# A fused attention, rotation and expert kernel on one core: the order of its first batch's theta, token-mixing and attention work changed, with weights staged by halves and some softmax sums kept in PSUM

## Chip, cores and metric

One core of one Trainium2 chip runs the whole program. The metric is device time in microseconds (us), the median of several executions. TensorE, VectorE, ScalarE, GpSimd and SyncE are called PE, DVE, ACT, POOL and SP in the rows.

## The reference

Three stages follow each other, for 4 batches of 576 tokens: a sparse attention of 8 heads (4 local, 4 strided), a rotation and mixing block, and four experts with causal attention. The change touches only the first two, and their order.

```python
scores = scale * np.matmul(q, k.transpose(0, 1, 3, 2))
scores = np.where(masks, scores, -1000000000.0)
attn = np.exp(scores - np.max(scores, axis=-1, keepdims=True))
attn = attn / (np.sum(attn, axis=-1, keepdims=True) + 1e-09)
x = np.matmul(attn, v)
...
theta = x @ w_theta
zr, zi = x * np.cos(theta), x * np.sin(theta)
y = np.einsum('ts,bsd->btd', w_tok_r, zr) + np.einsum('ts,bsd->btd', w_tok_i, zi)
u = x + y
x = u + np.maximum(u @ w_ch, 0.0)
```

The weights of the mixing block arrive as 64-bit floats.

## The kernel before

Every large product is done as three matmuls on a high and a low part of both factors (`mm3`, lines 252 to 255), so each weight is first split. `load64` (line 116) does it for `wth` (theta), `wtk` (token mixing) and `wch` (channel mixing): a chunk of 128 rows comes by DMA into a free part of the activation buffer X[3], ACT takes its magnitude (line 130), DVE builds the 32-bit pattern in three steps (lines 131 to 133) in X[2], ACT writes the high part (line 98) and DVE or POOL the low part (lines 100, 102). `wtk` has nine chunks and is loaded in two column halves.

Attention goes by pairs of heads, four per batch, each in three groups (`attn_pair`, line 161): scores on PE into a PSUM tile `s`, softmax on DVE and ACT (with ACT summing as it takes exponentials in the groups that `per_tile` names; DVE adds 1e-9 at line 203 and takes the reciprocal at 204), the division on POOL (205), a transposition `tp`, its copy `pt`, and the product with v into `av`, which is copied into X.

Then, per batch and column half h: `theta` (line 263) makes five tiles `th`, of twelve matmuls each, with two PSUM buffers; DVE takes a tile out into `cs` (lines 276, 277), ACT the absolute value (278) and, after the last tile, the cosines and sines (283, 284), for which it loads another table than for exponentials. `rotate` (286) multiplies with the transposed x and splits into `zhi` (ACT in the first batch) and `zlo` (POOL, 314). `tokens` (318) makes four tiles `y` of 27 matmuls per half. `channels` follows in the next batch.

The attention of batch b+1 is spread between these steps of batch b (`next_pair`, line 376; the main loop is lines 382 to 417). Within an engine a scheduler orders the instructions by readiness in a timeline of its own, starting from program order; each engine then works its list strictly in that order. `tc.issue_after(i)` puts the block's instructions behind instruction i on i's own engine only. All loads go through SP's one list.

In the first batch the order before is: attention of batch 0, with `wth` loaded after its first two pairs; theta half 0; rotation half 0; first half of `wtk`; theta half 1; rotation half 1; second half of `wtk`; pairs 0 and 1 of batch 1; `y` of half 0; `wch` and pair 2; pair 3; `y` of half 1.

Of the kernel before, what the change touches and what calls it, by code (L numbers as in the profile page):

```python
# [12 lines left out]
F32 = mybir.dt.float32  # L13
# [28 lines left out]
def fused_kernel(ctx: ExitStack, tc: tile.TileContext, ql, kl, vl, qs, ks, vs, wth, wtk, wch, wqk, wvg, wo, out):  # L42
# [73 lines left out]
    def load64(dst, src, kt, n0, n1, scale=1.0):  # L116
# [6 lines left out]
        slots = S // n  # L123
        for c in range(kt):
            raw = X[3].bitcast(U32).rearrange("p (a c) s -> p a (c s)", a=2)[:, c // slots % 2, :]
            raw = raw.rearrange("p (a s) -> p a s", a=slots)[:, c % slots, :2 * n].rearrange("p (n t) -> p n t", t=2)
# [6 lines left out]
            nc.vector.scalar_tensor_tensor(w, up, 0x80000000, w, op0=ALU.bitwise_and, op1=ALU.bitwise_or)  # L133
            split_w(hi[:, c, n0:n1], lo[:, c, n0:n1], st, scale, nc.vector if c % 3 == 1 else nc.gpsimd)

# [25 lines left out]
    def attn_pair(b, pair, ps1, apl, deep):  # L161
# [6 lines left out]
        for g, (j0, j1) in enumerate(groups):  # L168
# [13 lines left out]
            sm = apl.tile([128, 4], F32, tag="sm", name=f"sm_{b}_{pair}_{g}")  # L182
            p = apl.tile([128, 3 * LK], F32, tag="p", name=f"p_{b}_{pair}_{g}")
# [7 lines left out]
            if per_tile(b, pair, g):  # L191
                nc.vector.tensor_reduce(mx[:rm, :n], tiles(s), axis=AX.X, op=ALU.max, negate=True)
                nc.scalar.activation(mx[:rm, :n], mx[:rm, :n], AF.Copy, scale=SCALE)
                for i in range(n):
                    nc.scalar.activation(p[:rm, i * kw:(i + 1) * kw], s[:rm, i * kw:(i + 1) * kw], AF.Exp,
                                         bias=mx[:rm, i:i + 1], scale=SCALE, accum_out=sm[:rm, i:i + 1])
# [6 lines left out]
            nc.vector.tensor_scalar_add(sm[:rm, :n], sm[:rm, :n], 1e-9)  # L203
# [59 lines left out]
    def theta(b, h):  # L263
# [4 lines left out]
        for t in range(NT):  # L268
# [5 lines left out]
            cs = rp.tile([128, 2, 256], F32, tag="cs", name=f"cs_{b}_{h}_{t}")  # L274
# [85 lines left out]
    with tc.tile_pool(name="ps0", bufs=2, space=PSUM) as ps0, tc.tile_pool(name="ain0", bufs=9) as ain0, \  # L360
            tc.tile_pool(name="apl0", bufs=5) as apl0:
        for pair in range(4):
            load_pair(0, pair, ain0, 4, 4)
        attn_pair(0, 0, ps0, apl0, 2)
        attn_pair(0, 1, ps0, apl0, 2)
        load64(wth_s, wth, 4, 0, DM, INV2PI)
        for pair in range(2, 4):
            attn_pair(0, pair, ps0, apl0, 2)
    zu = ph1.enter_context(tc.tile_pool(name="zu", bufs=4))
# [12 lines left out]
    for b in range(B):  # L382
# [4 lines left out]
        rotate(b, 0)  # L387
        if b > 0:
            next_pair(b, 1)
        else:  # L390
            load64(wtk_s, wtk, 9, 0, HALF)
            load_pair(1, 0, ain, 2, 2)
        theta(b, 1)
        if b > 0:
            next_pair(b, 2)
        rotate(b, 1)
        if b == 0:
            load64(wtk_s, wtk, 9, HALF, S)
# [9 lines left out]
        if b == 0:  # L408
            next_pair(b, 0)
            next_pair(b, 1)  # L410
        tokens(b, 0)
        if b == 0:
            with tc.issue_after(sins[0, 1]):
                load64(wch_s, wch, 4, 0, DM)
# [312 lines left out]
```

## Time and profile before

| | us |
|---|---|
| median of 3 runs | 582.23 |
| lowest, highest | 581.08, 583.97 |
| the profiled execution | 579.94 |
| its span | 578.2 |
| PE busy in the span | 542.3 (94%) |
| DVE busy | 412.3 (71%) |
| ACT busy | 316.2 (55%) |
| POOL busy | 234.3 (41%) |
| mean granted clock of PE | 0.968 |

A row of a timeline gives an instruction's start, its length, its tile and, in brackets, how long the engine stood idle before it and what ended that. The clock column of a window is the granted clock of PE as a share of 2.4 GHz; 0.50 is the lower level, 1.2 GHz. A busy share over the whole span hides that the first fifth of it is worked differently from the rest.

### The profile page before, as it was taken

What the parts mean: (1) busy time and instruction counts of PE and PEld (TensorE: products, weight loads), DVE (VectorE), ACT (ScalarE), POOL (GpSimd) and SP (SyncE); (2) the same over time, 40 slices, a digit from 0 to 9 for tenths busy, and PEclk for the clock granted to TensorE, in tenths of its full rate; (3) what the DMA queues carried; (4) which work ended last, traced back from release to release, by engine and by line L of the source; (5) the groups of instructions that cost most, each with busy time, mean ns of one, the idle gap of its engine ahead of it and who ended that gap; (6) DMA issues with size and microseconds to landing.
All of it is one profiled execution on the core that took longest, in us unless ns stands there. A gap on an engine that the chain in (4) does not pass through costs nothing.

```text
span 578.2 us, 12507 instructions
## 1 busy us (share of the span) xinstructions
PE 542.3 (94%) x4560; PEld 508.1 (88%) x4560; DVE 412.3 (71%) x1205; ACT 316.2 (55%) x882; POOL 234.3 (41%) x314
## 2 busy tenths in 40 slices
PE   6787689899999999999999999899999999999996
PEld 6677579799999999999999999898989899899985
DVE  4896897995687456776255553488987888879882
ACT  5754966533536217254142550287678667866873
POOL 3532383650145211445104460365364534534452
PEclk9957969899999999999999999999999999999999
DMA  9557634221322013110100010100001001100012
GB/s 306 191 166 226 224 123 133 95 69 64 95 86 85 2 32 126 37 38 2 56 1 1 1 57 0 37 2 2 1 12 43 31 1 43 34 9 12 32 42 82
DMA packets 18660, 37.53 MB, mean 65 GB/s; under 512 B 2200, under 2 KB 9544, under 8 KB 18600
## 3 DMA queue, kind: packets, MB, share of 16 engines
q1 hardware_dynamic: 18600, 36.74, 19.6%
q8 instruction: 36, 0.59, 0.4%
q14 instruction: 24, 0.20, 0.1%
HBM read 32.01 MB, written 4.72 MB: 64 GB/s over the span
## 4 chain that ended last, share of the span: by engine, by line
PE 67%; DVE 14%; ACT 9%; DMA 5%; issue 2%; POOL 2%; SPq 0%; ACTq 0%; POOLq 0%; DVEq 0%
PE y L253 6%; PE y L254 6%; PE y L255 6%; PE tp L559 3%; PE th L253 3%; PE th L255 3%; PE th L254 3%; PE g L253 2%; PE g L254 2%; PE s L180 2%; PE g L255 2%; PE pq L253 2%; PE o L583 2%; PE s L533 2%; PE av L231 2%
## 5 line engine op out<-in xcount | busy, mean ns | idle before, releaser
L253 PE MATMUL y<-wtk_hi,zhi 128*128 128x288 f32 x288 | 86.9, 303 | 1.6 <-DVE cs L277 0.6
L254 PE MATMUL y<-wtk_lo,zhi 128*128 128x288 f32 x288 | 85.6, 298 | 1.0 <-POOL wtk_lo L100 1.0
L255 PE MATMUL y<-wtk_hi,zlo 128*128 128x288 f32 x288 | 84.5, 296 | 0.0
L314 POOL TENSOR_TENSOR zlo<-cs,zhi 128x512 fp32r<-128x512 f32 (+1 forms) x40 | 49.5, 1249 | 66.0 <-DVE zhi L311 42.1
L556 POOL TENSOR_SCALAR p<-p,sm,gt 128x256 f32<-128x256 f32 (+1 forms) x64 | 45.2, 709 | 57.2 <-DVE sm L554 38.9
L205 POOL TENSOR_TENSOR p<-p,sm 128x288 f32<-128x288 f32 (+2 forms) x48 | 32.3, 682 | 81.0 <-DVE sm L204 60.1
L549 ACT ACTIVATE p<-s,nm 128x128 f32<-128x128 f32 (+2 forms) x96 | 49.5, 517 | 14.8 <-DVE nm L538 10.0
L253 PEld LDWEIGHTS y<-wtk_hi,zhi 128*128 128x128 f32 x288 | 54.2, 188 | 3.0 <-DVE X L329 1.1
L249 POOL TENSOR_TENSOR x_lo<-X,x_hi 128x576 fp32r<-128x576 f32 x24 | 37.0, 1546 | 45.9 <-DVE x_hi L247 35.9
L254 PEld LDWEIGHTS y<-wtk_lo,zhi 128*128 128x128 f32 x288 | 54.2, 188 | 1.3 <-POOL wtk_lo L100 1.1
L255 PEld LDWEIGHTS y<-wtk_hi,zlo 128*128 128x128 f32 x288 | 53.9, 188 | 0.0
L253 PE MATMUL th<-wth_hi,x_hi 128*128 128x256 f32 (+1 forms) x160 | 50.2, 314 | 2.4 <-DVE cs L277 1.5
L538 DVE TENSOR_REDUCE nm<-s 128x1 f32<-128x128 f32 (+2 forms) x96 | 44.4, 469 | 5.2 <-PE s L536 3.9
L254 PE MATMUL th<-wth_lo,x_hi 128*128 128x256 f32 (+1 forms) x160 | 47.5, 297 | 0.0
L255 PE MATMUL th<-wth_hi,x_lo 128*128 128x256 f32 (+1 forms) x160 | 47.4, 297 | 0.0
L180 PEld LDWEIGHTS s<-k,q 128*108 128x108 f32 (+1 forms) x320 | 41.6, 201 | 6.0 <-issue 4.5
L180 PE MATMUL s<-k,q 128*108 128x54 f32 (+2 forms) x320 | 43.4, 279 | 3.4 <-DMA k<-in_kl 3.3
L253 PE MATMUL pq<-x_hi,wqk_hi 128*128 128x288 f32 x128 | 39.9, 312 | 0.7 <-DVE q L505 0.7
L212 ACT COPY pt<-tp 96x384 f32<-96x384 f32 (+2 forms) x44 | 20.8, 473 | 35.4 <-PE tp L208 35.2
L568 DVE TENSOR_TENSOR ptlo<-tp,pthi 128x128 fp32r<-128x128 f32 (+4 forms) x80 | 38.0, 478 | 2.5 <-ACT pthi L567 1.9
L253 PE MATMUL g<-u_hi,wch_hi 128*128 128x288 f32 x128 | 39.4, 308 | 0.2 <-DVE X L351 0.2
L254 PE MATMUL pq<-x_lo,wqk_hi 128*128 128x288 f32 x128 | 37.9, 296 | 0.0
(156 smaller groups left out, 1732.7 us busy)
## 6 DMA issues: line engine op xcount, KB each, us to landing
X<-in_wtk SPq DMA_DIRECT2D x18, 288.0 KB
q<-in_qs SPq DMA_DIRECT2D x8, 594.0 KB
q<-in_ql SPq DMA_DIRECT2D x8, 576.0 KB
out_t<-X SPq DMA_DIRECT2D x32, 144.0 KB
v<-in_vl SPq DMA_DIRECT2D x24, 144.0 KB
k<-in_kl SPq DMA_DIRECT2D x8, 304.0 KB
k<-in_ks SPq DMA_DIRECT2D x8, 288.0 KB
X<-in_wth SPq DMA_DIRECT2D x4, 512.0 KB
```

The costliest lines, as they stand in the source:

```text
L180: nc.tensor.matmul(s[:rm, i * kw:i * kw + w], qt[:, j0 + i, :], kt[:, k0:k0 + w], start=False, stop=i == n - 1)
L205: nc.gpsimd.tensor_tensor(tiles(p), tiles(p), each(sm), op=ALU.mult)
L212: copy(pt[:kw, :n * rm], tp[:kw, :n * rm])
L249: eng.tensor_tensor(lo, x, f(hi), op=ALU.subtract)
L253: nc.tensor.matmul(ps, ahi, bhi, start=first, stop=False)
L254: nc.tensor.matmul(ps, ahi, blo, start=False, stop=False)
L255: nc.tensor.matmul(ps, alo, bhi, start=False, stop=last)
L314: nc.gpsimd.tensor_tensor(lo, zf, f(hi), op=ALU.subtract)
L538: nc.vector.tensor_reduce(nm[:w, t + ci:t + ci + 1], s[:w, :c1 - c0], axis=AX.X, op=ALU.max, negate=True)
L549: nc.scalar.activation(p[:w, c0:c1], scs[ci][:w, :c1 - c0], AF.Exp, bias=nm[:w, t:t + 1], scale=1.0, accum_out=acc)
L556: eng.tensor_scalar(p[:w, :kn], p[:w, :kn], sm[:w, t:t + 1], gt[:w, t, e:e + 1], op0=ALU.mult, op1=ALU.mult)
L568: nc.vector.tensor_tensor(dst(ptlo), src, f(dst(pthi)), op=ALU.subtract)
```

## The change

Theta's weights come in two halves of 256 columns: the first is loaded after pair 1 of batch 0 and ahead of the loads of pairs 2 and 3, the second after those pairs. They are staged in X[1], so that `wtk` in X[3] no longer waits for them; every chunk now has one of four slots of its own. `wch` is loaded by halves too. Theta half 1 directly follows theta half 0; for four of its five tiles `cs` lies in X[1]. `load64` returns the last DVE step, and the first pair of batch 1 is put behind it on DVE and behind the last `zhi` of half 0 on ACT. In the 13 groups of batches 0 and 1 in which ACT sums, the sums go into four spare columns of the PSUM tile `s` (nine groups of batch 0, four of batch 1); DVE reads them there.

```diff
-    def load64(dst, src, kt, n0, n1, scale=1.0):
+    def load64(dst, src, kt, n0, n1, place, scale=1.0):
...
-            raw = X[3].bitcast(U32).rearrange("p (a c) s -> p a (c s)", a=2)[:, c // slots % 2, :]
-            raw = raw.rearrange("p (a s) -> p a s", a=slots)[:, c % slots, :2 * n].rearrange("p (n t) -> p n t", t=2)
+            raw = X[place].bitcast(U32)[:, c % 4, :2 * n].rearrange("p (n t) -> p n t", t=2)
...
-            nc.vector.scalar_tensor_tensor(w, up, 0x80000000, w, op0=ALU.bitwise_and, op1=ALU.bitwise_or)
+            got = nc.vector.scalar_tensor_tensor(w, up, 0x80000000, w, op0=ALU.bitwise_and, op1=ALU.bitwise_or)
...
+        return got.ins
...
+            ss = s[:, 384:388] if per_tile(b, pair, g) else sm
...
-                                         bias=mx[:rm, i:i + 1], scale=SCALE, accum_out=sm[:rm, i:i + 1])
+                                         bias=mx[:rm, i:i + 1], scale=SCALE, accum_out=ss[:rm, i:i + 1])
...
-            nc.vector.tensor_scalar_add(sm[:rm, :n], sm[:rm, :n], 1e-9)
+            nc.vector.tensor_scalar_add(sm[:rm, :n], ss[:rm, :n], 1e-9)
...
-            cs = rp.tile([128, 2, 256], F32, tag="cs", name=f"cs_{b}_{h}_{t}")
+            if (b, h) == (0, 1) and t < 4:
+                cs = X[1][:, t, :512].rearrange("p (a c) -> p a c", a=2)
+            else:
+                cs = rp.tile([128, 2, 256], F32, tag="cs", name=f"cs_{b}_{h}_{t}")
...
-        for pair in range(4):
+        for pair in range(2):
             load_pair(0, pair, ain0, 4, 4)
         attn_pair(0, 0, ps0, apl0, 2)
         attn_pair(0, 1, ps0, apl0, 2)
-        load64(wth_s, wth, 4, 0, DM, INV2PI)
+        load64(wth_s, wth, 4, 0, 256, 1, INV2PI)
+        for pair in range(2, 4):
+            load_pair(0, pair, ain0, 4, 4)
         for pair in range(2, 4):
             attn_pair(0, pair, ps0, apl0, 2)
+        load64(wth_s, wth, 4, 256, DM, 1, INV2PI)
...
-        rotate(b, 0)
-        if b > 0:
+            rotate(b, 0)
             next_pair(b, 1)
+            theta(b, 1)
+            next_pair(b, 2)
         else:
-            load64(wtk_s, wtk, 9, 0, HALF)
+            theta(b, 1)
+            rotate(b, 0)
+            ready = load64(wtk_s, wtk, 9, 0, HALF, 3)
             load_pair(1, 0, ain, 2, 2)
-        theta(b, 1)
-        if b > 0:
-            next_pair(b, 2)
         rotate(b, 1)
         if b == 0:
-            load64(wtk_s, wtk, 9, HALF, S)
+            load64(wtk_s, wtk, 9, HALF, S, 3)
...
         if b == 0:
-            next_pair(b, 0)
+
+            with tc.issue_after(ready), tc.issue_after(turns[0, 0]):
+                next_pair(b, 0)
             next_pair(b, 1)
         tokens(b, 0)
         if b == 0:
             with tc.issue_after(sins[0, 1]):
-                load64(wch_s, wch, 4, 0, DM)
+                for n0 in range(0, DM, 256):
+                    load64(wch_s, wch, 4, n0, n0 + 256, 3)
```

Names in the orders below carry batch, pair or half, and group or tile: `q_0_2` is q of batch 0, pair 2; `X1`, `X2` and `X3` are the buffers of batches 1 to 3, used for staging. SP's list from the loads of pair 2 of batch 0 on, before:

```order
L152 DMA q_0_2_146<-in_qs 128x1188
L153 DMA k_0_2_147<-in_ks 128x576
L157 DMA v_0_2_0_150<-in_vs 54x512
L157 DMA v_0_2_1_152<-in_vs 54x512
L157 DMA v_0_2_2_154<-in_vs 54x384
L152 DMA q_0_3_156<-in_qs 128x1188
L153 DMA k_0_3_157<-in_ks 128x576
L128 DMA X3_101<-in_wth 128x1024 x2
L157 DMA v_0_3_0_160<-in_vs 54x512
L157 DMA v_0_3_1_162<-in_vs 54x512
L157 DMA v_0_3_2_164<-in_vs 54x384
L128 DMA X3_101<-in_wth 128x1024 x2
```

and of the change:

```order
L126 DMA X1_99<-in_wth 128x512 x4
L151 DMA q_0_2_354<-in_qs 128x1188
L152 DMA k_0_2_355<-in_ks 128x576
L156 DMA v_0_2_0_358<-in_vs 54x512
L156 DMA v_0_2_1_360<-in_vs 54x512
L156 DMA v_0_2_2_362<-in_vs 54x384
L151 DMA q_0_3_364<-in_qs 128x1188
L152 DMA k_0_3_365<-in_ks 128x576
L126 DMA X3_101<-in_wtk 128x576 x4
L126 DMA X1_99<-in_wth 128x512
L156 DMA v_0_3_0_368<-in_vs 54x512
L126 DMA X1_99<-in_wth 128x512
```

A half of `wth` moved ahead of pair 2, four chunks of `wtk` ahead of everything that waits for `wth`, and the second half of `wth` behind them. DVE's list where theta's first tile is taken out (`cs_0_0_0`), before:

```order
L131 TENSOR_SCALAR X2_100<-X2_100 128x288
L132 SCALAR_TENSOR_TENSOR X2_100<-X3_101,X2_100 128x288
L133 SCALAR_TENSOR_TENSOR X2_100<-X3_101,X2_100 128x288
L276 TENSOR_SCALAR cs_0_0_0_619<-th_0_0_0_606 128x256
L276 TENSOR_SCALAR cs_0_0_1_636<-th_0_0_1_623 128x256
L131 TENSOR_SCALAR X2_100<-X2_100 128x288
L277 SCALAR_TENSOR_TENSOR cs_0_0_0_619<-cs_0_0_0_619,th_0_0_0_606 128x256
L100 TENSOR_TENSOR wtk_lo_114<-X2_100,wtk_hi_113 128x288
L192 TENSOR_REDUCE mx_1_0_0_1019<-s_1_0_0_1014 128x3
L277 SCALAR_TENSOR_TENSOR cs_0_0_1_636<-cs_0_0_1_636,th_0_0_1_623 128x256
```

and of the change:

```order
L130 SCALAR_TENSOR_TENSOR X2_100<-X3_101,X2_100 128x288
L131 SCALAR_TENSOR_TENSOR X2_100<-X3_101,X2_100 128x288
L129 TENSOR_SCALAR X2_100<-X2_100 128x288
L280 TENSOR_SCALAR cs_0_0_0_647<-th_0_0_0_634 128x256
L100 TENSOR_TENSOR wtk_lo_114<-X2_100,wtk_hi_113 128x288
L130 SCALAR_TENSOR_TENSOR X2_100<-X3_101,X2_100 128x288
L280 TENSOR_SCALAR cs_0_0_1_664<-th_0_0_1_651 128x256
L281 SCALAR_TENSOR_TENSOR cs_0_0_0_647<-cs_0_0_0_647,th_0_0_0_634 128x256
L131 SCALAR_TENSOR_TENSOR X2_100<-X3_101,X2_100 128x288
L193 TENSOR_REDUCE mx_1_0_0_1043<-s_1_0_0_1038 128x3
L199 TENSOR_REDUCE mx_1_0_1_1065<-s_1_0_1_1060 128x3
```

Five chunks of `wtk` (steps into X2) stood ahead of `cs_0_0_0` before; now eight do and the ninth has begun, and the maxima `mx_1_0_0` and `mx_1_0_1` of batch 1 stand behind the last step of the ninth. ACT's list behind the sines of theta half 0, before:

```order
L201 ACTIVATE p_1_1_1_1139<-p_1_1_1_1139 128x288
L130 ACTIVATE X2_100<-X3_101 128x288
L313 CAST zhi_0_0_0_704<-cs_0_0_0_619 128x512
L193 ACTIVATE mx_1_2_0_1368<-mx_1_2_0_1368 108x4
L98 ACTIVATE wtk_hi_113<-X2_100 128x288
L212 COPY pt_1_0_2_1076<-tp_1_0_2_1072 96x384
L130 ACTIVATE X2_100<-X3_101 128x288
L313 CAST zhi_0_0_1_712<-cs_0_0_1_636 128x512
L201 ACTIVATE p_1_1_2_1160<-p_1_1_2_1160 128x288
L130 ACTIVATE X2_100<-X3_101 128x288
L313 CAST zhi_0_0_2_720<-cs_0_0_2_653 128x512
L212 COPY pt_1_1_0_1130<-tp_1_1_0_1126 96x384
```

and of the change:

```order
L128 ACTIVATE X2_100<-X3_101 128x288
L98 ACTIVATE wtk_hi_113<-X2_100 128x288 x2
L282 ACTIVATE X1_99<-X1_99 128x256
L317 CAST zhi_0_0_0_823<-cs_0_0_0_647 128x512
L98 ACTIVATE wtk_hi_113<-X2_100 128x288
L282 ACTIVATE X1_99<-X1_99 128x256
L317 CAST zhi_0_0_1_831<-cs_0_0_1_664 128x512
L128 ACTIVATE X2_100<-X3_101 128x288
L282 ACTIVATE X1_99<-X1_99 128x256
L317 CAST zhi_0_0_2_839<-cs_0_0_2_681 128x512
L98 ACTIVATE wtk_hi_113<-X2_100 128x288
```

The exponentials (`p`), copies (`pt`) and maxima of batch 1 that stood between the `zhi` of half 0 have moved behind the sines of half 1, which follow without a table load between; ACT loads two tables fewer in all. On PE the first two score tiles of batch 1 (`s_1_0_0`, `s_1_0_1`) stand between the second and the third tile of theta half 0 before and after; from there to the last tile of theta half 1 no other work of batch 1 is left on PE, where before much of three pairs stood; the other ten groups' scores now stand among the matmuls of `y`. The number of instructions is the same on PE; DVE has 29 more, ACT 14, POOL 3 and SP 8.

## Rows read from the trace of the kernel before

**Rows 1.** Windows of the four stages: busy us (x instructions) by engine, clock, DMA.

```profile
0.00:38.00 38.00, 28.09 (x293) 23.74 (x294) 26.62 (x78) 25.36 (x102) 16.38 (x31) 0.85 0.62 212
38.00:88.50 50.50, 40.00 (x311) 36.76 (x312) 42.94 (x116) 32.69 (x101) 24.08 (x25) 0.77 0.64 199
88.50:131.50 43.00, 39.56 (x348) 37.39 (x348) 36.79 (x75) 21.83 (x48) 23.40 (x19) 0.96 0.29 94
131.50:578.20 446.70, 434.68 (x3614) 410.20 (x3612) 305.94 (x938) 236.32 (x634) 170.40 (x240) 1.00 0.11 34
```

**Rows 2.** Windows inside them: the same columns.

```profile
0.00:20.00 20.00, 15.64 (x149) 14.14 (x149) 10.68 (x41) 11.94 (x54) 7.11 (x22) 1.00 0.88 305
28.00:37.70 9.70, 7.96 (x88) 5.95 (x86) 8.77 (x19) 7.29 (x17) 3.41 (x4) 0.50 0.30 96
37.70:54.00 16.30, 12.98 (x61) 12.38 (x62) 11.75 (x28) 7.04 (x22) 5.17 (x5) 0.60 0.91 277
63.60:71.90 8.30, 4.12 (x50) 3.23 (x48) 6.03 (x16) 8.26 (x21) 2.82 (x4) 0.96 0.72 233
71.90:81.40 9.50, 7.06 (x41) 6.43 (x42) 9.46 (x24) 7.05 (x23) 8.96 (x9) 0.50 0.32 83
```

**Rows 3.** TensorE timeline: start, us, instruction [idle before <- what ended it].

```profile
37.72 0.58 PE L253 MATMUL th<-wth_hi,x_hi 128*128 128x256 f32 x1 [0.84 <-ACT X L238]
...
46.52 2.15 PE L180 MATMUL s<-k,q 128*128 128x96 f32 x12 [2.46 <-DMA k<-in_kl]
...
49.51 0.58 PE L253 MATMUL th<-wth_hi,x_hi 128*128 128x256 f32 x1 [0.84 <-DVE cs L277]
...
54.63 0.80 PE L180 MATMUL s<-k,q 128*128 128x96 f32 x6
...
71.94 0.91 PE L231 MATMUL av<-pt,v 96*64 96x64 f32 x12 [2.97 <-ACT pt L212]
...
88.50 0.38 PE L253 MATMUL y<-wtk_hi,zhi 128*128 128x288 f32 x1
...
94.40 0.29 PE L253 MATMUL y<-wtk_hi,zhi 128*128 128x288 f32 x1
...
94.53 0.30 PE L254 MATMUL y<-wtk_lo,zhi 128*128 128x288 f32 x1
```

**Rows 4.** ScalarE timeline: a table load, sines of theta half 1, what follows.

```profile
62.88 1.28 ACT L283 ACT_TABLE_LOAD   x1
...
95.60 0.51 ACT L283 ACTIVATE cs<-cs,halfpi 128x256 f32<-128x256 f32 x1
...
99.16 0.64 ACT L130 ACTIVATE X<-X 128x512 f32<-128x512 f32 x1
```

**Rows 5.** SyncE timeline: transfers issued.

```profile
32.32 4.52 SPq L128 DMA_DIRECT2D X<-in_wtk  x4
...
37.87 0.43 SPq L153 DMA_DIRECT2D k<-in_kl  x1
```

**Rows 6.** VectorE groups by form, 0 to 130 us: xcount | busy us, mean ns.

```profile
L132 DVE SCALAR_TENSOR_TENSOR X<-X,X 128x288 uint32<-128x288 uint32 x18 | 8.8, 490 | 0.1
...
L203 DVE TENSOR_SCALAR sm<-sm 108x4 f32<-108x4 f32 x8 | 6.2, 781 | 0.0
...
L132 DVE SCALAR_TENSOR_TENSOR X<-X,X 128x512 uint32<-128x512 uint32 x8 | 6.0, 755 | 0.0
...
L203 DVE TENSOR_SCALAR sm<-sm 108x3 f32<-108x3 f32 x4 | 3.8, 950 | 0.0
...
L203 DVE TENSOR_SCALAR sm<-sm 128x3 f32<-128x3 f32 x14 | 3.1, 226 | 1.8 <-ACT p L195 1.6
```

**Rows 7.** Lines 203 and 276: duration ns min/median/max, first and last start us.

```profile
L203 DVE TENSOR_SCALAR sm<-sm x48: 129/162/1737, 8.8 to 264.8; 128x3 f32<-128x3 f32 x24, 108x4 f32<-108x4 f32 x16, 108x3 f32<-108x3 f32 x8
...
L276 DVE TENSOR_SCALAR cs<-th x40: 382/423/426, 47.4 to 318.9; 128x256 f32<-128x256 f32 x32, 64x256 f32<-64x256 f32 x8
```

**Rows 8.** Tile cs, line 314: the low part of z on GpSimd, ns min/median/max.

```profile
L314 POOL TENSOR_TENSOR zlo<-cs,zhi x10: 723/1354/1943, 71.2 to 116.8; 128x512 fp32r<-128x512 f32 x8, 128x256 fp32r<-128x256 f32 x2
```

More of the change, by code (lines that the diff above doesn't have):

```diff
@@ L114, in new_split @@
         return tuple(pool.tile([128, kt, n], F32R, name=f"{name}_{part}") for part in ("hi", "lo"))
-    def load64(dst, src, kt, n0, n1, scale=1.0):
+    def load64(dst, src, kt, n0, n1, place, scale=1.0):
         hi, lo = dst
         n = n1 - n0
-        slots = S // n
         for c in range(kt):
-            raw = X[3].bitcast(U32).rearrange("p (a c) s -> p a (c s)", a=2)[:, c // slots % 2, :]
-            raw = raw.rearrange("p (a s) -> p a s", a=slots)[:, c % slots, :2 * n].rearrange("p (n t) -> p n t", t=2)
+            raw = X[place].bitcast(U32)[:, c % 4, :2 * n].rearrange("p (n t) -> p n t", t=2)
             st = X[2][:, c % 4, :n]
```

## Prediction

> **What bounds the kernel now.** I read the span in slices and the granted clock first, then windows by stage, then the timeline of PE at the borders of the stages, and last the groups and timelines of the engines on which PE waits. PE is busy for most of the span, so I count what it loses: its idle time, plus half of its busy time in stretches where the clock is at the lower level (work at 1.2 GHz takes twice as long as at 2.4).
>
> By stage [rows 1, 2]: from 0 to 38 us (attention of batch 0) PE idles 9.9 us and has 7.96 us at clock 0.50, so it loses 9.9 + 4.0 = 13.9. From 38 to 88.5 (theta, three pairs of batch 1, until `y` starts) it idles 10.5 us; 12.98 us (37.7 to 54) and 7.06 us (71.9 to 81.4) lie mostly at the lower level, which costs 10.0: together 20.5. The first window's mean of 0.60 takes in idle time, so I count all of it. From 88.5 to 131.5 (first `y`) it idles 3.4 us and loses 0.04 x 39.6 = 1.6 to the clock: 5.0. Up to 131.5 that is 39.4 us lost and 131.5 - 39.4 = 92.1 us of work at full speed. Behind 131.5 PE idles 12.0 of 446.7 us at clock 1.00, and no line changes there. The change adds nothing to PE, so all that it can bring lies in these 39.4 us, and more than half in the theta stage.
>
> What holds PE there [rows 3, 4]: theta starts at 37.72; its third tile waits for DVE to empty a PSUM buffer (line 277), until 49.51; ahead of it a score tile of batch 1 waits 2.46 us for its `k` (46.52). Then score tiles of batch 1 and theta alternate, behind softmax work on DVE and ACT; the table for theta's sines is loaded at 62.88; `y` begins only at 88.50, with the second half's sines later still, at 95.60.
>
> **The change part by part.** *Stage A, until theta starts.* The first half of `wth` (4 x 256 KB = 1.05 MB) now goes ahead of the loads of pairs 2 and 3; at the 305 GB/s of the first 20 us [rows 2] that delays them by 3.4 us. In exchange half of the conversion of `wth` moves to where DVE was busy for 10.68 of 20 us, and away from 28 to 37.7, where DVE was busy for 8.77 of 9.7. Bounds: 2 us earlier to 3.4 later. I take 0: the end that is nearest to a row is the relief of DVE, which was nearly full just ahead of theta, but pair 3 comes later.
>
> *Third theta tile.* Before, four chunks of `wtk` were issued at 32.32, for 4.52 us, ahead of `k` at 37.87 [rows 5]. Now these four chunks (1.18 MB, 3.9 us at 305 GB/s) leave before the second half of `wth`, and more conversions stand ahead of `cs_0_0_0` on DVE. The last chunk of `wth` should land near 43.5 and take about 3 us to be converted and to let the tile go: 46.5 in place of 49.51. Bounds: 45.6 (little behind the landing) to 49.5 (no change). I take 46.5.
>
> *Theta to its sines.* From 49.51 to the table load at 62.88 were 13.4 us, with softmax of batch 1 on DVE and ACT between. Behind the hold some 3.3 us of it are gone from DVE, and theta tiles follow each other: I take about 10, so the table load comes near 56. A table load and the sines of both halves, 1.28 + 3.56 us for the ten of the second half [rows 4], end near 61. Four `zhi` on ACT, among conversions that wait, take about 5.4 by the spacing of the same work before: 66.6. `zlo` on POOL, 1.35 us each [rows 8], follows them. The first two tiles of `y` are 54 matmuls x 0.13 us (two starts, 94.40 and 94.53, [rows 3]) = 7 us; they should start near 64 and, waiting for `zlo` and for `wtk`, end near 73. That is as if `y` began whole at 66.5. So the stage runs from 38 to 66.5 = 28.5 us. Its work: 120 theta matmuls x 0.117 us (0.13 x 256/288) = 14, and 3 for two score tiles (0.80 each [rows 3]) and some transposes: 17. It loses 11.5, where before it lost 20.5.
>
> *First y stage.* What is left is 92.1 - 24.1 (stage A's 38 - 13.9) - 17 = 51.0 us of work, with more of batch 1's attention in it than before. DVE bounds this: it was busy 26.62 + 42.94 + 36.79 = 106.4 us up to 131.5 [rows 1]. Halves instead of whole rows add about 3: a step of 288 columns takes 490 ns and one of 512 takes 755 [rows 6], so two of 256 (estimated at 0.45 each) cost 0.15 us more, sixteen times, and the shorter operations of 16 chunks the rest. That makes 109, so by 124.5 DVE may idle for 15 us only, if it is to end there; before it idled for 25. I take 7 us lost by PE, against 5.0 before; bounds 3 (DVE out of the way) to 14 (the whole gain used up). The stage ends at 66.5 + 51.0 + 7 = 124.5, which is **7.0 us earlier** than 131.5.
>
> *Sums in PSUM.* Thirteen of line 203's instructions read PSUM instead of SBUF: eight of 128x3, four of 108x4, one of 108x3 [rows 6]. On SBUF their times run from 129 to 1737 ns; the nearest row with a PSUM operand (line 276, an addition of a scalar too) runs from 382 to 426 at 256 columns [rows 7]. If all come down from their means to the median of 162 ns, that saves 8 x 0.064 + 4 x 0.62 + 0.79 = 3.8 us of DVE. If PSUM costs 382 for the few columns too and the stalls only move to the next SBUF step, it loses 13 x 0.22 = 2.9. I take 0, as the reciprocal behind each stays in SBUF, and keep both ends inside the 3 to 14 us of the `y` stage. The same price lies in a sum that ACT adds up into PSUM instead of SBUF; the exponential itself already reads PSUM, so nothing is counted.
>
> *Table loads.* ACT loads two tables fewer, 2 x 1.28 = 2.6 us of ACT. ACT is busy 32.69 of 50.5 us in the theta stage, and what waits for it is counted above: 0 apart from that, at most 2.6. In the Trainium skill, "ScalarE: Activation LUTs", section "What ACT_TABLE_LOAD costs", a switch costs about 2.7 us with its drain, by which two fewer would be worth 5.3 in place of 2.6; the row here shows 1.28.
>
> *The rest at nothing.* The 8 more DMAs on SP are covered by SP's free time (DMA at 0.29 of its time from 88.5 [rows 1]); without the cover, 8 issues at 1.13 us (four took 4.52 [rows 5]) are 9 us of queue. Putting batch 1's first pair behind `ready` on DVE and the last `zhi` on ACT keeps its softmax back by some 15 us: two score tiles on PE then hold both `s` buffers, which theta and `y` don't need.
>
> **Sum.** The profiled execution takes 579.94 (span 578.2): 579.94 - 7.0 = 572.9. The median of the runs is 2.3 above that execution, so the forecast is **575.0**. Ends: with stage A 2 us earlier, the third theta tile 0.9 earlier and `y` losing 3 instead of 7 it is 7 less, 568; with `y` losing 14 there is no gain, 582; a third tile 3 us later alone gives 578, a stage A 3.4 later alone 578.4.
>
> **The rivals.**
>
> *The hold acts on DVE and ACT alone.* The order of PE still has two score tiles of batch 1 ahead of the third theta tile, and PE works its list in order. If their `k` comes as late as before, these end at 46.52 + 2.15 = 48.7 and theta's third tile can't start before: 2.2 later than taken, 577.2. For it: `k` was the wait before, for 2.46 us. Against: `q`, `k` of pair 0 may be asked for earlier. Chance 0.15.
>
> *DVE becomes the bound of the y stage.* Behind the third theta tile everything of batch 1 that was spread over 50 us falls into the stage of `y`, with `zlo` and divisions on POOL. SBUF-to-SBUF steps on DVE (eight sums left, eight steps of `wch`, casts) can stand behind a whole POOL operation of 1.35 us; line 203 shows it, with a minimum of 129 ns and a maximum of 1737, while line 276, on PSUM, never exceeds 426 [rows 7]. A dozen such waits at 1.35 - 0.16 = 1.2 use up the slack of some 8.5 us (of the 15, 6.6 lie in stage A: it idled 11.4 there, and four half chunks at about 1.2 take 4.8 of it) and push the end back by 5 (12 x 1.2 - 8.5 = 5.9, of which 1 is in the 7 lost): 580, no change. Against: before, these waits were as frequent and DVE idled 25 us all the same. Chance 0.17. The Trainium skill, "SBUF — State Buffer", section "Who interferes with whom", tells of a shared port pair with an exclusive lock between VectorE and GpSimd, which a PSUM operand escapes; the spread of line 203 against line 276 agrees with it.
>
> *Slower: the lower clock under theta and the first y.* From 46.5 to 73 lies 19.8 us of work (eight theta tiles x 12 x 0.117 = 11.2, 1.6 of other work, the 7 of `y`) in 26.5 us. Were all of it at 1.2 GHz it would take 39.6, 13.1 more than the window: 588. The window has 6.7 us of slack, so the gain of 7 is eaten once 6.7 + 7 = 13.7 of the 19.8 us, about 70%, run so. For it: between 63.6 and 71.9 PE was busy 4.12 of 8.3 us and then was granted 0.50 until 81.4 [rows 2], and theta's tiles still wait for PSUM buffers. Against: the clock was 0.96 in that same loose window, and 0.96 again in the first `y` stage. Chance 0.10.
>
> **How the numbers follow.** Forecast 0.58 (575.0), hold-not-on-PE 0.15 (577.2), DVE 0.17 (580), lower clock 0.10 (588). A measurement of this kernel tells about 0.5% from no change, 2.9 us. Faster (below 579.3): 0.58 + 0.15 = 0.73; within: 0.17; slower (above 585.1): 0.10. The range of 567 to 583 takes in the first three with the bounds of the sum, and leaves the last out.
>
> **What would show it.** Theta starts within 2 us of 37.7; its third tile near 46.5 and not behind a score tile that waits for `k`; one table load near 56 for the sines of both halves; the first `y` near 64 and its 54th matmul near 73; the last `y` matmul of half 1 near 124.5; line 203's PSUM form without times over 0.3 us; granted clock 1.00 from the first `y` on. I am wrong if theta starts 3 us later, if clock 0.50 reaches into the first `y`, or if DVE is busy without a gap from 66 to 124 and the end stays at 131.

## The result: slower by 0.7%, and the profile after

Over 11 runs each, the kernel before takes 583.56 us and the changed one 586.81: a ratio of 1.0073, with a 95% interval from 1.0046 to 1.0100. The forecast was 575.0, in a range of 567 to 583. The time lies above it, and the kernel is slower where it was to be faster. A ratio here is that of the means of two kernels' executions without those in a slower state (three of the twelve of `e4_sums_in_sbuf`, at most two elsewhere), so it can differ a little from what two medians give.

The profiled execution after took 586.81 us (span 585.0), the one shown of before 579.94, so these two are 6.9 us apart where the medians are 3.25 apart. A place that both pass far behind the change tells how much of it belongs to the change: the same matmul of `y`, behind the same wait of 0.42 us. Before, on TensorE's timeline:

```profile
341.36 0.40 PE L253 MATMUL y<-wtk_hi,zhi 128*128 128x288 f32 x1 [0.42 <-DVE X L329]
```

And after, TensorE's timeline at the starts of theta, of a score tile, of theta's third tile and of `y`, and at the same place:

```profile
42.52 0.58 PE L254 MATMUL th<-wth_hi,x_hi 128*128 128x256 f32 x1 [1.42 <-ACT X L239]
...
48.91 0.32 PE L179 MATMUL s<-k,q 128*128 128x96 f32 x1 [1.01 <-DMA k<-in_kl]
...
53.45 0.58 PE L254 MATMUL th<-wth_hi,x_hi 128*128 128x256 f32 x1 [2.99 <-DVE cs L281]
...
73.27 0.37 PE L254 MATMUL y<-wtk_hi,zhi 128*128 128x288 f32 x1 [1.28 <-ACT wtk_hi L98]
...
344.46 0.40 PE L254 MATMUL y<-wtk_hi,zhi 128*128 128x288 f32 x1 [0.42 <-DVE X L333]
```

By there the changed kernel is 3.1 us late, about what the medians say. Theta starts 4.8 us later than before and its third tile 3.9 later [rows 3]; `y` starts 15 us earlier, yet most of that is given back. The other 3.7 us of the two profiles arise behind this place, 3.4 of them in the two short windows at clock 0.50 below (half of 3.42 + 3.43 us of busy time), in lines that the change leaves alone; before, the last stage stood at 1.00 [rows 1]. Windows after: the three stages and the rest, then these two, with busy us by engine, clock, DMA share and GB/s, as in [rows 1]:

```profile
0.00:42.50 42.50, 29.87 (x292) 24.88 (x292) 31.53 (x104) 28.02 (x116) 17.20 (x32) 0.85 0.64 212
42.50:73.20 30.70, 22.15 (x142) 20.14 (x142) 27.33 (x63) 18.71 (x48) 11.78 (x12) 0.88 0.64 197
73.20:129.90 56.70, 50.28 (x455) 46.36 (x456) 48.31 (x118) 31.27 (x97) 28.33 (x32) 0.94 0.37 115
129.90:585.00 455.10, 440.58 (x3673) 415.80 (x3671) 310.83 (x951) 237.60 (x638) 173.89 (x244) 0.99 0.11 35
398.14:401.56 3.42, 3.42 (x17) 3.39 (x18) 2.81 (x13) 1.33 (x5) 1.67 (x3) 0.50 0.00 0
572.20:575.64 3.44, 3.43 (x16) 3.05 (x16) 0.45 (x1) 0.80 (x2) 1.22 (x3) 0.50 0.00 0
```

PE idles 12.6 us until theta starts (9.9 of 38 us before), and 6.4 us in the `y` stage, with DVE busy for 48.3 of 56.7.

Why the third tile waits until 53.45 is read backwards. On DVE, `cs_0_0_0` (line 280) stands behind a conversion step that waits for ACT (0.53 us):

```profile
51.35 0.31 DVE L129 TENSOR_SCALAR X<-X 128x288 uint32<-128x288 uint32 x1 [0.53 <-ACT X L128]
51.58 0.42 DVE L280 TENSOR_SCALAR cs<-th 128x256 f32<-128x256 f32 x1
```

and on ACT that step waits for a chunk of `wtk`:

```profile
50.86 0.46 ACT L128 ACTIVATE X<-X 128x288 f32<-128x288 f32 x1 [1.84 <-DMA X<-in_wtk]
```

That chunk is the ninth of `wtk`. SyncE's timeline shows why it comes so late: the first four chunks are issued from 14.12 on, the fifth only at 38.25 and the ninth at 44.78, since each needs a slot that DVE's conversion has to free first; the ninth goes out behind the fifth's last step on DVE, at 44.27.

```profile
14.12 3.29 SPq L126 DMA_DIRECT2D X<-in_wtk  x4
...
21.59 1.64 SPq L126 DMA_DIRECT2D X<-in_wth  x2
38.25 3.43 SPq L126 DMA_DIRECT2D X<-in_wtk  x3
...
44.78 0.33 SPq L126 DMA_DIRECT2D X<-in_wtk  x1
```

The wait for it is short, though: from 38 to 51.58 us DVE is busy for 12.5 of 13.6 us. Most of the lateness is the conversion steps themselves that stand ahead of `cs_0_0_0` on DVE: 25 on `wtk`, against 15 before.

### The profile page after: what moved, and what is told of

Same layout as the page of the kernel before. It is cut to its first block, busy times and chain, and to the rows that moved or that the text cites. A ratio compares the mean times of both kernels' runs of the same rounds, so it can differ in the third digit from the quotient of the medians.

```text
span 585.0 us, 12584 instructions
## 1 busy us (share of the span) xinstructions
PE 542.9 (93%) x4560; PEld 507.2 (87%) x4560; DVE 418.0 (71%) x1234; ACT 315.6 (54%) x896; POOL 231.2 (40%) x317
## 4 chain that ended last, share of the span: by engine, by line
PE 72%; DVE 15%; ACT 6%; DMA 3%; issue 2%; POOL 1%; SPq 0%; POOLq 0%; ACTq 0%; DVEq 0%
PE y L254 6%; PE y L255 6%; PE y L256 6%; PE s L179 5%; PE tp L569 3%; PE av L232 3%; PE th L254 3%; PE g L254 3%; PE g L256 2%; PE g L255 2%; PE th L256 2%; PE th L255 2%; PE tp L209 2%; PE o L593 2%; PE pq L254 2%
## 5 line engine op out<-in xcount | busy, mean ns | idle before, releaser
L256 PE MATMUL y<-wtk_hi,zlo 128*128 128x288 f32 x288 | 85.8, 300 | 0.0
L206 POOL TENSOR_TENSOR p<-p,sm 128x288 f32<-128x288 f32 (+2 forms) x48 | 30.8, 647 | 95.9 <-DVE sm L205 56.0
L318 POOL TENSOR_TENSOR zlo<-cs,zhi 128x512 fp32r<-128x512 f32 (+1 forms) x36 | 43.0, 1206 | 57.7 <-DVE zhi L315 43.5
L559 ACT ACTIVATE p<-s,nm 128x128 f32<-128x128 f32 (+2 forms) x96 | 49.5, 517 | 14.8 <-DVE nm L548 10.5
L254 PE MATMUL th<-wth_hi,x_hi 128*128 128x256 f32 (+1 forms) x160 | 48.8, 306 | 7.5 <-DVE cs L281 4.5
L256 PE MATMUL th<-wth_hi,x_lo 128*128 128x256 f32 (+1 forms) x160 | 46.6, 293 | 0.0
L255 PE MATMUL th<-wth_lo,x_hi 128*128 128x256 f32 (+1 forms) x160 | 46.6, 292 | 0.0
L254 PEld LDWEIGHTS th<-wth_hi,x_hi 128*128 128x128 f32 (+1 forms) x160 | 30.2, 189 | 9.2 <-DVE cs L281 5.5
```

What stands on the lines that cost most here:

```text
L206: nc.gpsimd.tensor_tensor(tiles(p), tiles(p), each(sm), op=ALU.mult)
L254: nc.tensor.matmul(ps, ahi, bhi, start=first, stop=False)
L255: nc.tensor.matmul(ps, ahi, blo, start=False, stop=False)
L256: nc.tensor.matmul(ps, alo, bhi, start=False, stop=last)
L318: nc.gpsimd.tensor_tensor(lo, zf, f(hi), op=ALU.subtract)
L559: nc.scalar.activation(p[:w, c0:c1], scs[ci][:w, :c1 - c0], AF.Exp, bias=nm[:w, t:t + 1], scale=1.0, accum_out=acc)
```

## The experiments

The kernel before ran beside each of them; its median moved between 581.6 and 582.2. Ratios are to those runs.

**First round: conversions ahead of attention, or the hold?** On DVE of the changed kernel, six steps on `wtk` run ahead of pair 3's copy `pt` (none before) and 25 ahead of the first `cs` (15 before); the expectations below say three and 14, since they count entries of an instruction list, and only the two-input steps. My first theory was that this order delays theta and loses the time; the rival, that the hold does.

`e1_wtk_behind_pair3`:

```diff
-            ready = load64(wtk_s, wtk, 9, 0, HALF, 3)
+            with tc.issue_after(copied[0, 3, 1]):
+                ready = load64(wtk_s, wtk, 9, 0, HALF, 3)
```

> The change, with the conversions of wtk's first half put behind pair 3's copy pt on DVE (before it three of their steps stood ahead of that copy, and 14 ahead of the first cs; now 0 and 5). Stage theory (the change loses because conversions of weights stand ahead of pair 3 of batch 0 and of cs_0_0_0 on DVE, so that theta starts 4.8 us later and its third tile 3.9 us later): theta starts at 39 to 41 in place of 42.5, the third tile at 44 to 49 in place of 53.5, and the time is 582 to 584.5. Hold theory (the loss comes from batch 1's softmax, which is held back and then meets a full DVE from 73 to 104 us): 586 to 588, as with the change, however early theta starts.

582.51 us, 1.0010 [0.9984, 1.0037]. Theta starts at 39.09, its third tile at 50.55, a little later than expected. That agrees with the first theory: with every sum left in PSUM, an order on DVE without `wtk` ahead of pair 3 gives back 0.6%.

`e2_wth_whole`:

```diff
-        load64(wth_s, wth, 4, 0, 256, 1, INV2PI)
-        for pair in range(2, 4):
-            load_pair(0, pair, ain0, 4, 4)
+        load64(wth_s, wth, 4, 0, DM, 1, INV2PI)
...
-        load64(wth_s, wth, 4, 256, DM, 1, INV2PI)
```

> The change, with wth loaded whole and behind the loads of all four pairs, as before the change (staged in X[1], two slots). Stage theory: theta starts at 37.5 to 40 in place of 42.5, the third tile near 50, the time is 582 to 584.5. Hold theory: 586 to 588. If halves were a help, as predicted, it is slower than the change.

578.78 us, 0.9941 [0.9913, 0.9969]: better than expected, though theta starts at 40.64 only. This kernel, too, has every sum in PSUM.

`e3_no_hold`:

```diff
-            with tc.issue_after(ready), tc.issue_after(turns[0, 0]):
-                next_pair(b, 0)
+            next_pair(b, 0)
```

> The change without the hold: batch 1's first pair is bound neither to the last conversion step nor to the last zhi. Stage theory: theta starts at 42.5 as with the change, and the time is 586 to 589, since softmax of batch 1 comes back among theta's tiles. Hold theory: 582 to 584.5, with DVE less full from 73 to 104 us.

587.65 us, 1.0101 [1.0063, 1.0139]. The hold theory falls: without it the kernel is no faster.

`e4_sums_in_sbuf`:

```diff
-            ss = s[:, 384:388] if per_tile(b, pair, g) else sm
+            ss = sm
```

> The change with all row sums in SBUF again. The scheduler's order changes with it: no conversion step of wtk stands ahead of pair 3's copy any more (three did), and 12 in place of 14 ahead of the first cs. Stage theory: theta starts at 40 to 41.5 in place of 42.5 and the time is 584 to 586. If the sums in PSUM save DVE the 3.8 us that their stalls cost before, it is 587 to 590. Hold theory: 586 to 588.

579.33 us, 0.9932 [0.9903, 0.9961]. None of the theories had this: the smallest part of the change, taken out, turns 0.7% of loss into 0.7% of gain. TensorE's timeline of this kernel at the places of above:

```profile
39.22 0.58 PE L254 MATMUL th<-wth_hi,x_hi 128*128 128x256 f32 x1 [1.59 <-ACT X L239]
...
49.66 0.39 PE L254 MATMUL th<-wth_hi,x_hi 128*128 128x256 f32 x1 [1.38 <-DVE cs L281]
...
65.56 0.38 PE L254 MATMUL y<-wtk_hi,zhi 128*128 128x288 f32 x1
...
334.64 0.41 PE L254 MATMUL y<-wtk_hi,zhi 128*128 128x288 f32 x1 [0.42 <-DVE X L333]
```

**Second round: which sums, and is it the order that comes with them?** The scheduler's order shifts with where the sums lie, so the order could still be the cause. Taking the sums of one batch at a time leaves the early order of DVE as it was in one case and not in the other.

`e5_sums_psum_batch0` and `e6_sums_psum_batch1`, one line each:

```diff
-            ss = s[:, 384:388] if per_tile(b, pair, g) else sm
+            ss = s[:, 384:388] if per_tile(b, pair, g) and b == 0 else sm
```

> The change with only batch 0's nine sums in PSUM, batch 1's four in SBUF. The order of DVE up to theta half 0 is that of the change (three steps of wtk ahead of pair 3's copy, 14 ahead of the first cs). Order theory (the sums cost nothing by themselves; by what the scheduler reckons for them it puts conversions ahead of pair 3 and of cs, and that costs): theta starts at 42 to 43, 585 to 588, as with the change. Tile theory (a sum in PSUM keeps the score tile s until DVE has read it, and batch 1 has only two s tiles, so PE's scores wait): most of the loss is batch 1's, so 579 to 582.

> The change with only batch 1's four sums in PSUM, batch 0's nine in SBUF. The order of DVE up to the first y tiles is that with all sums in SBUF (no step of wtk ahead of pair 3's copy). Order theory: theta starts at 39 to 40, 578 to 581.5. Tile theory: 584 to 588.

580.14 us, 0.9981 [0.9955, 1.0007], and 582.61 us, 1.0012 [0.9984, 1.0040]. The first has the changed kernel's order up to theta, starts theta at 41.22, and still keeps most of the gain: the order theory falls as an account of the whole loss, though not of the part that `e1_wtk_behind_pair3` gave back. The second lies between its two expected ranges. Each batch's sums cost a part (0.5% and 0.8% against 0.9932), and the parts make about the 1.4% of both. The four sums of batch 1 leave theta where it was (38.88 against 39.22) and cost behind the start of `y` (65.77 against 65.56): at the common place the kernel is at 340.61 against 334.64, in one profiled execution of each (that of `e4_sums_in_sbuf` took 576.43, 2.9 less than its median).

`e7_pairs_first`: the loads of pairs 2 and 3 back ahead of `wth`, halves and sums as in the change.

```diff
-        for pair in range(2):
+        for pair in range(4):
             load_pair(0, pair, ain0, 4, 4)
...
-        for pair in range(2, 4):
-            load_pair(0, pair, ain0, 4, 4)
```

> The change with all 13 sums in PSUM and wth in halves, but the loads of all four pairs ahead of wth, as before the change. No step of wtk stands ahead of pair 3's copy on DVE, 11 ahead of the first cs (14 with the change). Order theory: theta starts at 38 to 40.5, 578 to 582, though every sum is in PSUM. Tile theory: 585 to 588, as the sums are where the change has them.

585.41 us, 1.0056 [1.0026, 1.0085], theta at 41.25. With no step of `wtk` ahead of pair 3's copy it is as slow as the change, within the intervals: a second miss for the order theory as the whole account.

`e8_wth_whole_sums_sbuf` takes the edits of `e2_wth_whole` and `e4_sums_in_sbuf` together.

> The change with wth whole and all sums in SBUF: what is left is theta's halves in a row, the hold and wch in halves. Two steps of wtk ahead of pair 3's copy, 9 ahead of the first cs. Order theory: theta starts at 38.5 to 40.5; each of the two edits gave back the loss alone, so together no more than the better of them: 576 to 580. Tile theory: 574 to 577, the two gains added (8 and 4 us).

583.15 us, 1.0022 [0.9997, 1.0047]: neither. Two edits that each gain lose it together. From theta on until 85 us its ACT loads six tables, of 1.28 us each, where `e4_sums_in_sbuf` loads two. Four of the six:

```profile
73.48 1.28 ACT L200 ACT_TABLE_LOAD   x1
75.85 1.28 ACT L291 ACT_TABLE_LOAD   x1
...
80.43 1.28 ACT L200 ACT_TABLE_LOAD   x1
82.51 1.28 ACT L291 ACT_TABLE_LOAD   x1
```

Exponentials (line 200) have come between the sines (291). Whether that is all of it was not tried. Four of these kernels make a table of two by two:

| | `wth` in halves | `wth` whole |
|---|---|---|
| sums in PSUM | 1.0073 [1.0046, 1.0100] (the change) | 0.9941 [0.9913, 0.9969] (`e2_wth_whole`) |
| sums in SBUF | 0.9932 [0.9903, 0.9961] (`e4_sums_in_sbuf`) | 1.0022 [0.9997, 1.0047] (`e8_wth_whole_sums_sbuf`) |

Beside halves of `wth` the sums in PSUM cost 1.4%; beside whole rows they gain 0.8%. So in the changed kernel the loss takes both parts together, and taking out either gives back as much. It is the halves rather than the order of the loads, as `e7_pairs_first` moved the loads alone and gained nothing clear. Why, the runs don't show; the scheduler makes another order in each of the four.

**What a sum in PSUM does.** ScalarE's list of the changed kernel, with what each instruction waits for, has the second to fourth exponential of a group wait for ACT itself, and other work in between:

```
L196 ACTIVATE p_0_3_1_512,s_0_3_1_504<-s_0_3_1_504,mx_0_3_1_510 108x54 [waits Activation_49,Pool_49]
L194 ACTIVATE mx_0_3_2_544<-mx_0_3_2_544 108x3 [waits DVE_49]
...
L128 ACTIVATE X2_100<-X1_99 128x256 [waits DMAHW1_49]
L196 ACTIVATE p_0_3_1_512,s_0_3_1_504<-s_0_3_1_504,mx_0_3_1_510 108x54 [waits Activation_49]
```

Each exponential writes its sum into the tile that the next one reads, so the program makes them a chain. ScalarE's timelines show it. The first group before (a short step reads out the sum behind each exponential):

```profile
7.67 0.34 ACT L195 ACTIVATE p<-s,mx 128x96 f32<-128x96 f32 x1
7.91 0.19 ACT L195 ACTIVATION_READ_ACCUMULATOR p<-s,mx 128x1 f32 x1
8.00 0.33 ACT L195 ACTIVATE p<-s,mx 128x96 f32<-128x96 f32 x1
...
8.31 0.34 ACT L195 ACTIVATE p<-s,mx 128x96 f32<-128x96 f32 x1
```

and after, the first group and, at 83 us, batch 1's first:

```profile
8.27 0.34 ACT L196 ACTIVATE p<-s,mx 128x96 f32<-128x96 f32 x1
8.51 0.16 ACT L196 ACTIVATION_READ_ACCUMULATOR p<-s,mx 128x1 f32 x1
8.70 0.34 ACT L196 ACTIVATE p<-s,mx 128x96 f32<-128x96 f32 x1
...
9.13 0.34 ACT L196 ACTIVATE p<-s,mx 128x96 f32<-128x96 f32 x1
...
83.25 0.34 ACT L196 ACTIVATE p<-s,mx 128x96 f32<-128x96 f32 x1
...
83.54 0.46 ACT L128 ACTIVATE X<-X 128x288 f32<-128x288 f32 x1
83.90 0.34 ACT L196 ACTIVATE p<-s,mx 128x96 f32<-128x96 f32 x1
...
84.17 0.43 ACT L98 ACTIVATE wch_hi<-X 128x256 fp32r<-128x256 f32 x1
84.48 0.46 ACT L202 ACTIVATE p<-p 128x288 f32<-128x288 f32 x1
84.81 0.36 ACT L196 ACTIVATE p<-s,mx 128x96 f32<-128x96 f32 x1
```

The exponentials start 0.43 us apart where they follow each other, against 0.32, though each lasts as long as before; elsewhere conversions stand between them. Batch 1's first group takes 1.56 us from its first start to its last, where `e4_sums_in_sbuf` takes 0.64 (77.89 to 78.53). The sum also keeps the score tile until DVE has read it.

**Third round: the sums alone, and what in them.** All four are the kernel before, three with one edit and the last with two. Starts of theta are from one profiled execution each.

`e9_before_sums_psum`: the sums in PSUM, as in the change.

> The kernel before with the 13 groups' sums in PSUM and nothing else changed. Chain theory (in PSUM each exponential of a group waits for the one before it, since its sum lies in the tile that the next one reads; they start 0.43 us apart in place of 0.32, and the scheduler puts conversions between them): the first groups' exponentials start 0.43 us apart, and the time is 584.5 to 590, slower than before. Stall theory (PSUM operands spare DVE the stalls of the sums): 578 to 581. No effect by itself: 581 to 583.

586.53 us, 1.0082 [1.0050, 1.0114]: put into the kernel before by themselves, the sums lose as much as the whole change does. Its first exponentials start at 7.47, 7.90 and 8.34, and theta starts at:

```profile
43.33 0.58 PE L254 MATMUL th<-wth_hi,x_hi 128*128 128x256 f32 x1 [2.69 <-ACT X L239]
```

`e13_before_chained_exps`: the chain without PSUM.

```diff
-                    nc.scalar.activation(p[:rm, i * kw:(i + 1) * kw], s[:rm, i * kw:(i + 1) * kw], AF.Exp,
+                    e = (i + 1) * kw + (i < n - 1)
+                    nc.scalar.activation(p[:rm, i * kw:e], s[:rm, i * kw:e], AF.Exp,
```

> The kernel before, sums in SBUF, but each exponential of a group but the last takes one column more, which the next one overwrites (so its sum has one exponential too many: a changed computation). The exponentials of a group are so chained without a sum in PSUM. Chain theory: they start 0.43 us apart, conversions come between them in ACT's order, and the time is 584.5 to 589, as with the sums in PSUM (586.5). Place theory (it is PSUM that costs, as the place of the sum or by the score tile that is held longer): 581 to 584, as with the kernel before.

583.56 us, 1.0032 [1.0003, 1.0060]. The first exponentials start at 7.65, 8.12 and 8.58, and theta as late as with the sums in PSUM:

```profile
43.51 0.58 PE L254 MATMUL th<-wth_hi,x_hi 128*128 128x256 f32 x1 [2.38 <-ACT X L239]
```

So in the kernel before the chain is enough to make theta late (its links are 0.46 us here), but by the ratios it brings under half of the loss, and its expected 584.5 to 589 was missed. In the changed kernel the chain alone does not make theta late: `e1_wtk_behind_pair3` has it too and starts at 39.09.

`e14_before_score_held` holds the score tile, and `e15_before_chain_and_held` does both.

```diff
-            nc.vector.tensor_scalar_add(sm[:rm, :n], sm[:rm, :n], 1e-9)
+            if per_tile(b, pair, g):
+                nc.vector.scalar_tensor_tensor(sm[:rm, :n], s[:rm, :n], 0.0, sm[:rm, :n], op0=ALU.mult, op1=ALU.add)
+            else:
+                nc.vector.tensor_scalar_add(sm[:rm, :n], sm[:rm, :n], 1e-9)
```

> The kernel before, sums in SBUF, but in the 13 groups DVE's step on the sum also reads the score tile in PSUM (times zero, added to the sum; the 1e-9 is left out there), so that the tile is held until then, as with a sum in it. Held theory (what the chain alone did not lose, 1.0082 against 1.0032, is the score tile held longer): 584 to 587. Order theory (the rest is what the scheduler makes of both, not the holding): 581 to 583.5, theta starting near 38.

> Both: the exponentials of a group chained by the column that overlaps (sums with one exponential too many) and the score tile held until DVE's step on the sum. If chain and holding are all that the sums in PSUM do: 585 to 588, theta at 43 to 44, as with the sums in PSUM (1.0082). If PSUM as the place matters besides, or the rest is the scheduler's order: 582.5 to 584.5, as with the chain alone.

583.46 us, 1.0018 [0.9994, 1.0042], and 585.52 us, 1.0066 [1.0043, 1.0089]. Holding alone can't be told from no change. Whether it makes theta late stays open: its one profiled execution starts theta at 43.44, where near 38 or later was the question, but took 589.69 us, 6 above the median, with TensorE's clock at 0.50 earlier than before. With both, theta starts at 42.72, near the 43 to 44 expected; chain and holding together lose what the sums in PSUM lose, within the intervals (1.0066 against 1.0082). How much of it is the waits themselves, and how much the order that the scheduler builds upon them, the runs don't part.

**What the rest of the change is worth**, with the sums in SBUF (0.9932):

`e10_sbuf_halves_apart`: `rotate(b, 0)` and the first half of `wtk` again written between the halves of theta.

> The change with all sums in SBUF and theta's halves apart again: the rotation of half 0 and the first half of wtk stand between them, the hold stays. If the row is what gains (579.3 with it, theta's sines of both halves behind one table load): 582 to 586, and y begins later than at 66. If the hold alone gains: 578 to 581.

579.15 us, 0.9943 [0.9911, 0.9976]. No difference: `y` starts at 65.54 and there is one table load for both halves' sines even so. The scheduler makes the row by itself once the hold is there.

`e11_sbuf_no_hold`: the edit of `e3_no_hold`.

> The change with all sums in SBUF and no hold. If the hold is what gains: 582 to 586, with softmax of batch 1 among theta's tiles and more table loads before y. If the row alone gains: 578 to 581.

581.25 us, 1.0007 [0.9975, 1.0039], between the two expected ranges: the hold is worth some 0.7% by the ratios, less by the medians (579.33 and 581.25). Without it a second load for the sines comes at 80.19 us, and `y` starts at 76.60.

`e12_sbuf_wch_whole`:

```diff
-                for n0 in range(0, DM, 256):
-                    load64(wch_s, wch, 4, n0, n0 + 256, 3)
+                load64(wch_s, wch, 4, 0, DM, 3)
```

> The change with all sums in SBUF and wch loaded whole. The prediction's count (shorter steps cost DVE about 1.5 us for wch's eight halves, where DVE is full): 577 to 579. If halves only let the chunks flow earlier: 580 to 583.

574.84 us, 0.9878 [0.9846, 0.9910]: the best version of all, faster than both kernels, and faster than expected. The halves of `wch` cost some 3 us (0.9932 against 0.9878, with intervals that just touch). Its profiled execution took 580.19, far above its median, so nothing is read from it.

## Why the prediction was wrong

**The step that failed** stands under "Sums in PSUM": "The same price lies in a sum that ACT adds up into PSUM instead of SBUF; the exponential itself already reads PSUM, so nothing is counted." I priced the operand on DVE and forgot what the new place makes wait: the next exponential on ACT, and whoever wants the score tile next. Counted at 0, with ends of 2.9 lost and 3.8 gained, it cost 1.4% in the changed kernel (1.0073 against 0.9932), some 8 us of the 11.8 between forecast and result. The kernel before loses 0.8% by the same edit alone (1.0082), and 0.7% by a chain and a held score tile without PSUM (1.0066). But the loss is not the sums' alone: with `wth` whole they gain (0.9941 against 1.0022). So a second part was mis-sized beside them, the halves of `wth`: they cost 1.3% with sums in PSUM and gain 0.9% with sums in SBUF, and no term of the sum had the two together. Why they act on each other stays open.

What I did price there came out in part. DVE's steps with the sum in PSUM never stall. Line 204 after (duration ns min/median/max):

```profile
L204 DVE TENSOR_SCALAR sm<-sm x35: 136/160/1229, 23.5 to 277.9; 128x3 f32<-128x3 f32 x16, 108x4 f32<-108x4 f32 x12, 108x3 f32<-108x3 f32 x7
L204 DVE TENSOR_SCALAR sm<-s x13: 143/149/161, 9.6 to 120.8; 128x3 f32<-128x3 f32 x8, 108x4 f32<-108x4 f32 x4, 108x3 f32<-108x3 f32 x1
```

That the stalls then move to the next SBUF steps is borne out best by `e9_before_sums_psum`, where only the sums moved: up to 130 us the steps that add 1e-9 take 6.1 us of DVE in place of 13.1, and the two-input conversion steps 34.9 in place of 29.9. Their groups there (busy us, mean ns; at line 132 before 490 and 755 ns [rows 6]):

```profile
L133 DVE SCALAR_TENSOR_TENSOR X<-X,X 128x288 uint32<-128x288 uint32 x18 | 10.8, 597 | 0.0
L132 DVE SCALAR_TENSOR_TENSOR X<-X,X 128x288 uint32<-128x288 uint32 x18 | 9.4, 527 | 0.1
L132 DVE SCALAR_TENSOR_TENSOR X<-X,X 128x512 uint32<-128x512 uint32 x8 | 8.1, 1027 | 0.0
...
L133 DVE SCALAR_TENSOR_TENSOR X<-X,X 128x512 uint32<-128x512 uint32 x8 | 6.6, 834 | 0.0
...
L204 DVE TENSOR_SCALAR sm<-s 128x3 f32<-128x3 f32 x8 | 1.2, 152 | 0.8 <-ACT p L196 0.7
```

In the changed kernel these steps of 288 columns take longer too (593 ns at what is now line 130), but they take 576 with the sums in SBUF again, so there it is mostly not the sums' doing.

**Stage A**, taken as 0 with an upper end of 3.4: theta starts 4.8 us later, at 42.52. Without the sums in PSUM (`e4_sums_in_sbuf`, here and below "without the sums") it is 1.5 (39.22). I looked for room on DVE in the first 20 us. PE's longest wait just ahead of theta, 3.22 us until 39.39, ends with pair 3's copy `pt`: the row names ACT, but its matmuls read `pt`, whose copy ends on DVE at 39.29. That copy stands among the conversion steps of `wtk`, which the change brought ahead of it. TensorE's wait, and the copy on DVE:

```profile
39.39 1.71 PE L232 MATMUL av<-pt,v 54*64 54x54 f32 x28 [3.22 <-ACT wtk_hi L98]
```

```profile
38.70 0.59 DVE L213 COPY pt<-tp 54x432 f32<-54x432 f32 x1
```

With these steps behind the copy (`e1_wtk_behind_pair3`) theta starts at 39.09, so here most of the lateness goes with this order. It comes with the sums in PSUM: with all of them in SBUF the scheduler puts no step of `wtk` ahead of the copy.

**Third tile**, 46.5 with an upper end of 49.5: 53.45, and 49.66 without the sums. I had counted conversions ahead of `cs_0_0_0` and given them 3 us behind a landing at 43.5, a chunk of `wth`. The last chunk of `wth` was issued by 23.2 us. The chunk that counted was the ninth of `wtk`, whose slot DVE freed so late that ACT had it only at 50.86, and ahead of that DVE was full with steps on the others. A list of instructions shows who stands ahead; it does not show that one of them waits for a transfer that waits for the same engine.

**Theta to its sines**, table load near 56 and `y` from 64: 63.74 and 73.27; without the sums 57.57 and 65.56. From the third tile to the table load that is 10.3 us against 10 predicted, and 7.9 without the sums: the mechanism of the hold was read rightly, behind a late start (without hold, in `e11_sbuf_no_hold`, it is 11.3).

**First y stage**, its 54th matmul near 73 and the last near 124.5: 83.46 and 129.84; without the sums 80.13 and 118.81. The term of 7 us that PE loses had DVE as its reason, and DVE is indeed full, 27.87 of 28 us from 82 to 110 (23.39 before). Without the sums 0.7% was gained of the 1.2% forecast. That 574.8 with `wch` whole lies at the forecast of 575.0 is luck: it is another kernel, and the forecast had the halves of `wch` in it.

**The rivals.** The hold on DVE and ACT alone: the score tile's `k` did come late (a wait of 1.01 us, at 48.91), but the third tile waited for DVE until 53.45, so that cost nothing. DVE as the bound: DVE was full there, but the reason I gave, SBUF steps that stand behind POOL, speaks for sums in PSUM, and those were part of the loss. It did occur once: PE's longest wait in the `y` stage, 2.34 us until 98.60, goes back over a conversion step to a sum left in SBUF that took 1.23 us on DVE (96.08 to 97.31) while a `zlo` of 1.30 us ran on POOL (95.99 to 97.29). The lower clock: PE ran at 0.50 from 29.5 to 46.6, from 53.4 to 56.8 and, inside the first `y` stage, from 97.8 to 104.6. So this sign came true, but the 5.12 us that PE was busy in the last stretch cost 2.6 us against 1.6 before; the theory's cost of 13 did not come. The sign "theta starts 3 us later" came true as well, by 4.8. The side with 0.10 came, by a mechanism that was not on the list.

## What to carry to other kernels

Before an output is moved into a tile that already has readers and writers, list every instruction that touches this tile: the move adds an edge to each, and a group that ran back to back can become a chain that a scheduler fills with other work. An order by readiness hides such an edge; look for it as waits on the engine itself and for starts that lie further apart. And measure a change of several parts with each part taken out, and then with two taken out: here the part counted at zero outweighed the one that was meant to gain, and beside another form of a third part the same part gained.

## What the runs showed of the hardware

A chained exponential of 128x96 on ScalarE starts 0.43 us behind the one before, an unchained one 0.32, at the same duration of 0.34; in these first groups the step that reads out its sum takes 0.16 us into PSUM and 0.19 to 0.20 into SBUF, so the shorter step is in the slower group. In the unchained group the next exponential starts at 8.00, before the read-out of 7.91 with its 0.19 has ended; in the chained one it starts at 8.70, after 8.51 + 0.16: what is lost is this overlap of some 0.1 us. The Trainium skill, "ScalarE: Activation LUTs", section "What ACT_TABLE_LOAD costs", says that back-to-back activations overlap by about 93 ns; the rows of before agree, and a link of the chain takes it away.

In the first microseconds matmuls ran at about half of their later rate for longer after than before, though the granted clock stands at 1.00 there in both. The same six score matmuls take, before and after:

```profile
11.38 0.80 PE L180 MATMUL s<-k,q 128*128 128x96 f32 x6
```

```profile
13.73 1.43 PE L179 MATMUL s<-k,q 128*128 128x96 f32 x6
```

The rows don't say why, and what it cost was not parted from the rest; by 30 us both kernels have run about as many matmuls (228 after, 227 before); with the sums in SBUF (`e4_sums_in_sbuf`) twelve of these matmuls, at 10.13 us, take 2.85, as slow, so it is not the sums' doing. The two stretches at clock 0.50 near 398 and 572 us appear near 392 and 566 also in the profiled execution of `e5_sums_psum_batch0`, which is faster than the changed kernel; PE was busy without a gap inside them, and no cause was found.
